# Splitting one head pair of the scores across the boundary of a woven cycle

## The chip, the cores and the metric

The kernel runs on one core of a Trainium2 chip. The metric is the device time of one execution in microseconds, the median of several runs. Before the change it is 1395.99 us (three runs, 1395.55 to 1398.74).

## The reference

A pre-norm transformer block on one sequence of 2048 tokens with width 512. Attention has 32 heads of 16 with a single key and value head shared by all; the feed-forward part is a gated GELU with 1792 hidden features. Everything is float32.

```python
q = (x @ wq).reshape(B, S, 32, 16).transpose(0, 2, 1, 3)
k = x @ wk
v = x @ wv
p = softmax(einsum("bhqd,bkd->bhqk", q, k) * 16 ** -0.5)
o = einsum("bhqk,bkd->bhqd", p, v).transpose(...).reshape(B, S, 512) @ wo

h = x + attention(layernorm(x))
h2 = h + (gelu(layernorm(h) @ w_gate) * (layernorm(h) @ w_up)) @ w_down
```

## The kernel before

**Blocks and groups.** The 2048 queries are worked in four blocks `b` of 512 columns. In a block the 32 heads come in eight groups `g` of four, and for each group the 2048 keys come in 16 chunks `kc` of 128. One iteration `i` is one (block, group, chunk): four heads, in two pairs `u = 0, 1`. There are 512 iterations and 1024 pairs, numbered by `n` (`i, u = divmod(n, 2)`).

**A score** (`scores`, L370): two matmuls, one for each head `a` of the pair. Each has 50 contraction rows, the first at partitions 0 to 49, the second at 64 to 113, so that the two stand in different row halves of TensorE and run at the same time. They write the two banks of one PSUM tile `s` (128 keys x 2 x 512 queries). ScalarE then takes the exponential of the whole tile, 1024 columns in one instruction (L374), into half of a tile `p` in SBUF. There are two `s` tiles (pool `pss`, four banks) in the woven part, and five `p` tiles.

**A weigh** (`weigh`, L378): for one iteration, four matmuls of 32 columns side by side multiply the four heads' `p` by the values and add to the accumulator `acc` (one bank). In the trace each of the four is two records. An iteration can be weighed when both of its exponentials are done. The list `pend` holds iterations that are scored but not yet weighed, and `finish(n)` weighs the `n` oldest.

**A dense step** (`step`, `rows`, L827): output projection, up projections and down projections of the block before the one in attention. Each product of 128 contraction rows is cut in two halves of 64 rows, the "firsts" in rows 0 to 63 and the "seconds" in rows 64 to 127, which go to different PSUM banks and are added by VectorE. A step issues one matmul of a first and one matmul of a second, which run at the same time; the seconds lag six steps behind (`LAG`). A product is mostly 12 steps long, so a product's half ends every six steps. When it ends, VectorE copies or adds its bank (`done`: L690, L694, L757, L615, L618), and up to two more VectorE instructions that wait in the list `later` are issued (`side`). There are three banks for products; two are in use at a time, and the list `spare` hands them out in the order in which they came free.

**The weave.** `CYCLES` sets the order by hand. A cycle has a number of weighs, all at its beginning, then a string of moves, `s` a score and `d` a dense step, and a second string for cycles in which too few dense steps are available (`idle`), where weighs and scores alternate:

```python
CYCLES = (
    (3, "ssdddddsdddsddds", "vssvssvs"),
    (3, "ssdddddsdddsddds", "vssvssvs"),
    (2, "ssdddddsdddsdddsddds", "ssvssvss"),
)
```

Three cycles make a repeat: 8 weighs, 16 scores, 36 dense steps. Before each cycle `before` issues what ScalarE and VectorE have to do beside it (the gate's tanh, L706; the divisions by the sums, L414; the turning of normalized rows). A tanh stands on ScalarE ahead of the cycle's exponentials. The order on TensorE, ScalarE and GpSimd is as written; SyncE and VectorE too in this part.

**What comes before and after.** The first block's attention and 23 scores of the second (`lead`) run without dense work; there a third tile `s3` serves the scores as well, and a few weighs alternate with scores. The last block's dense part follows the weave in an order of its own (L865).

Of the kernel before, what the change touches and what calls it, by code (L numbers as in the profile page):

```python
# [9 lines left out]
F32 = mybir.dt.float32  # L10
# [3 lines left out]
AF = mybir.ActivationFunctionType  # L14
# [5 lines left out]
P = 128  # L20
# [22 lines left out]
LAG = 6  # L43
# [16 lines left out]
def kernel(  # L60
# [12 lines left out]
    nc = tc.nc  # L73
# [6 lines left out]
    T = 512  # L80
# [8 lines left out]
    KR = 3 * DH + 2  # L89
    SCALE = float(DH) ** -0.5  # L90
# [21 lines left out]
    kaug = const.tile([P, S], F32R, name="kaug")  # L112
# [45 lines left out]
    def run(outer, first):  # L158
# [204 lines left out]
        def scores(i, p, qg, kc, u):  # L363

            third = width == 1 and (2 * i + u) % 3 == 2
            pool, tag, bufs = (ps, "s3", 1) if third else (pss, "s", 2)
            s = pool.tile([P, 2, T], F32, tag=tag, bufs=bufs, name=f"s_{i}_{u}")
            for a in range(2):
                rows = slice(64 * a, 64 * a + KR)
                nc.tensor.matmul(  # L370
                    s[:, a, :], kaug[rows, kc * P : (kc + 1) * P], qg[rows, u, :],
                    start=True, stop=True,
                )
            nc.scalar.activation(p[:, 2 * u : 2 * u + 2, :], s, AF.Exp, scale=SCALE)  # L374

        def weigh(acc, p, kc):
            for j in range(4):
# [84 lines left out]
        late = ExitStack()  # L462
# [95 lines left out]
        scaled_at, halves, gs, gated = {}, {}, {}, set()  # L558
# [246 lines left out]
        left = [0]  # L805
        built = []

        def rows(a):
            nonlocal at
            i = 0  # L810
            while i < len(queue):
                name, n, terms, done, ready = queue[i]
                i += 1
                if a == 0:
                    assert ready is None or ready()
                    left[0], at = n, i
                    built.append([])
                    source = iter(terms())
# [3 lines left out]
                for k in range(n):  # L822
                    if a == 0:
# [3 lines left out]
                    nc.tensor.matmul(  # L827
                        bank, lhsT[r], rhs[r], start=(k == 0), stop=(k == n - 1),
                        skip_group_check=True,
                    )  # L830
                    if k == n - 1:
                        spare.append(tag)
                        done(a, bank)
                        side(2)
                    yield

        def step(first=True):
            nonlocal ahead, clock
            clock += 1
            if first and next(firsts, 0) is None:  # L840
                ahead += 1
            if ahead > LAG or not first:
                assert ahead > 0
                next(seconds)
                ahead -= 1

        tail_banks = ["acc", "t3", "d", "d", "d", "t0", "t1", "t2"]

# [195 lines left out]

        cur = {}

        def score(n):

            nonlocal acc
            i, u = divmod(n, 2)  # L1050
            b, r = divmod(i, PER)
            g, kc = divmod(r, KC)
            if u == 0:
                if kc == 0:
                    cur["qg"] = qgs.pop((b, g))
                    acc = psa.tile([P, T], F32, tag="acc", bufs=1, name=f"acc_{b}_{g}")
                if kc == 2 and b * NG + g + 1 < NB * NG:
                    key = divmod(b * NG + g + 1, NG)
                    qgs[key] = load_q(*key)
                cur["p"] = sb.tile([P, 4, T], F32, tag="p", bufs=PB, name=f"p_{i}")  # L1060
            scores(i, cur["p"], cur["qg"], kc, u)
            if u == 1:
                pend.append((b, g, kc, cur["p"], acc, n))

        banks.close()
# [67 lines left out]
        assert not outs  # L1133
        set_banks("ps_rest")
# [7 lines left out]
        def before(idle):  # L1142
# [21 lines left out]
        fixed.enter_context(  # L1164
            tc.manual_schedule(engines={mybir.EngineType.SP, mybir.EngineType.DVE})
        )
        for i in range(-((lead - end) // 16)):
            if first and i in BOUND_LISTS:
                bound_flag(BOUND_LISTS.index(i))
            for count, woven, plain in CYCLES:  # L1170
                idle = available() < woven.count("d")
                if idle:
                    while available():
# [10 lines left out]
                for move in plain if idle else woven:  # L1184
                    if move == "d":
                        step()
                    elif move == "v":
                        if n == end and not last_x:
                            prepare_x()
                        finish(1)  # L1190
                        clock += 4
                    elif n < end:
                        score(n)
                        n += 1
                        clock += 1
        fixed.close()
        assert not pend and not outs and at == len(queue) and left[0] == 0
        held_banks.close()
# [383 lines left out]
```

## Time and profile before

| | |
|---|---|
| median of the runs | 1395.99 us |
| the profiled execution's own time | 1397.61 us |
| span in its trace | 1395.8 us |
| granted TensorE clock | 1.00 |
| weighs (L378), 4096 records | 490.0 us busy |
| scores (L370), 1984 records of the main shape | 388.3 us busy |
| exponentials (L374), 1024 | 959.6 us busy, 1037 ns each |
| tanh of the gate (L706), 42 | 27.8 us busy, 662 ns each |

The profile is a hardware trace of one execution. PE is TensorE's matmuls, PEld its weight loads, which overlap matmuls; DVE is VectorE, ACT ScalarE, POOL GpSimd. A row of the timeline has the start in us from the span's beginning, the time from the start of the first to the end of the last of the instructions merged in it, engine, line, operation, output and inputs, shapes, the count, and in brackets the idle time before it and what ended it. A row of a group has the busy time in all, the mean of one instruction in ns, and the idle time of the engine just before them with what ended most of it. Matmuls are pipelined: one of 512 columns is recorded with about 0.39 us, but the next can start before it ends, so the distance between starts tells the rate. Some matmul records may be missing.

### The profile page before, as it was taken

The page shows a single profiled execution, that of the slowest core. Times are in us where ns is not written, and L with a number is a line of the kernel's source. Part 1 is how long each engine was busy: PE and PEld are TensorE (multiplying, and loading weights), DVE is VectorE, ACT ScalarE, POOL GpSimd, SP SyncE. Part 2 cuts the span into 40 slices and gives each one's busy share as a digit, 9 for nine tenths or more (in the row PEclk, how much of TensorE's full clock was granted, in tenths as well). Part 3 has the DMA queues.
Part 4 walks back from the last instruction along what each step waited for, and adds up shares of the span by engine and source line. Part 5 has one row for each costly group of instructions (what it writes and reads, how often), then busy time and mean ns, then how long its engine had stood idle before and what let it go on. Part 6 is the DMA issues. An engine that isn't in the chain of part 4 may idle for free.

```text
span 1395.8 us, 25287 instructions
## 1 busy us (share of the span) xinstructions
PE 1379.5 (99%) x10406; PEld 753.3 (54%) x10406; DVE 651.0 (47%) x1097; ACT 1034.1 (74%) x1157; POOL 239.8 (17%) x346
## 2 busy tenths in 40 slices
PE   9999999999999999999999999999999999999998
PEld 7533333325555555545555555545555555558886
DVE  7413131314354444548364444448364453546665
ACT  8799999997787777877787777787778777772000
POOL 7576777621000000002000000001000000011000
PEclk9999999999999999999999999999999999999999
DMA  5565776753232333311522433321433333233552
GB/s 163 167 216 184 235 235 233 220 181 133 73 106 74 118 104 103 116 60 46 181 94 81 134 103 103 104 66 31 148 103 104 118 103 103 91 123 126 187 205 94
DMA packets 66783, 180.32 MB, mean 129 GB/s; under 512 B 9672, under 2 KB 9672, under 8 KB 66628
## 3 DMA queue, kind: packets, MB, share of 16 engines
q1 hardware_dynamic: 55324, 143.29, 31.0%
q0 software_dynamic: 10208, 35.26, 7.6%
q8 instruction: 84, 1.38, 0.4%
q14 instruction: 39, 0.32, 0.1%
q10 hardware_dynamic: 1128, 0.07, 0.1%
HBM read 130.87 MB, written 47.45 MB: 128 GB/s over the span
## 4 chain that ended last, share of the span: by engine, by line
PE 94%; ACT 2%; DMA 1%; DVE 1%; issue 1%; SPq 0%; POOL 0%; ACTq 0%; POOLq 0%
PE acc L378 33%; PE s L370 20%; PE pg L827 9%; PE pu L827 8%; PE pd L827 7%; PE pq L219 3%; PE pd L865 3%; PE pg L865 3%; PE pu L865 3%; PE pp L827 2%; ACT p L374 2%; PE pp L929 1%; PE pd_rest L877 1%; DMA x<-in_A_x_dram 1%; PE pk L1327 1%
## 5 line engine op out<-in xcount | busy, mean ns | idle before, releaser
L374 ACT ACTIVATE p<-s 128x1024 f32<-128x1024 f32 x1024 | 959.6, 1037 | 223.7 <-PE s L370 220.6
L378 PE MATMUL acc<-p,v_sb 128*32 128x512 f32 x4096 | 490.0, 598 | 0.0
L370 PE MATMUL s<-qg,kaug 50*128 50x512 f32 x1984 | 388.3, 426 | 4.2 <-ACT p L374 4.1
L370 PEld LDWEIGHTS s<-qg,kaug 50*128 50x128 f32 x1984 | 169.4, 184 | 281.7 <-ACT p L374 123.5
L378 PEld LDWEIGHTS acc<-p,v_sb 128*32 128x32 f32 x4096 | 108.7, 109 | 233.1 <-issue 218.7
L827 PE MATMUL pg<-x2h,w 64*128 64x512 f32 x672 | 175.2, 392 | 0.0
L827 PE MATMUL pu<-x2h,w 64*128 64x512 f32 x672 | 174.5, 392 | 0.0
L827 PE MATMUL pd<-w,gh 64*128 64x512 f32 x624 | 124.7, 394 | 1.9 <-DVE h L615 1.6
L757 DVE TENSOR_TENSOR h<-h,pd 128x512 f32<-128x512 f32 x80 | 55.0, 687 | 140.7 <-PE pd L827 140.6
L137 POOL TENSOR_SCALAR rstd<-mv 128x1 f32<-128x1 f32 x16 | 3.6, 223 | 649.1 <-DVE mv L135 648.8
L827 PEld LDWEIGHTS pg<-x2h,w 64*128 64x128 f32 x672 | 95.5, 186 | 11.4
L827 PEld LDWEIGHTS pu<-x2h,w 64*128 64x128 f32 x672 | 95.7, 186 | 10.8
L827 PE MATMUL pg<-x2l,w 64*128 64x512 f32 x336 | 99.9, 392 | 0.0
L827 PE MATMUL pu<-x2l,w 64*128 64x512 f32 x336 | 99.9, 391 | 0.0
L827 PEld LDWEIGHTS pd<-w,gh 64*128 64x128 f32 x624 | 69.7, 185 | 15.0 <-DVE h L615 2.5
L391 DVE COPY oT<-acc 128x512 f32<-128x512 f32 x32 | 22.1, 692 | 112.5 <-PE acc L378 112.3
L983 ACT ACTIVATE ga<-ga 128x512 f32<-128x512 f32 x14 | 8.8, 632 | 88.5 <-DVE ga L980 88.5
L827 PE MATMUL pd<-w,gl 64*128 64x512 f32 x312 | 72.1, 392 | 0.0
L694 DVE TENSOR_TENSOR g<-g,pg 128x512 f32<-128x512 f32 x42 | 28.8, 685 | 90.8 <-PE pg L827 90.8
L414 DVE RECIPROCAL oc<-oc 128x128 f32<-128x128 f32 x64 | 56.7, 923 | 21.4 <-DMA oc<-acc_d 17.6
L690 DVE COPY g<-pg 128x512 f32<-128x512 f32 x42 | 29.1, 692 | 72.0 <-PE pg L827 72.0
L694 DVE TENSOR_TENSOR u<-u,pu 128x512 f32<-128x512 f32 x42 | 28.8, 686 | 68.6 <-PE pu L827 68.6
(255 smaller groups left out, 1493.1 us busy)
## 6 DMA issues: line engine op xcount, KB each, us to landing
w<-w_d SPq DMA_DIRECT2D x126, 512.0 KB
w<-w_d SPq DMA_DIRECT2D x21, 1024.0 KB
qg<-q_d SPq DMA_DIRECT2D x62, 200.0 KB
q_d<-qh SPq DMA_DIRECT2D x32, 256.0 KB
acc_d<-oT SPq DMA_DIRECT2D x31, 256.0 KB
oc<-acc_d SPq DMA_DIRECT2D x124, 64.0 KB
w_d<-w_0b POOLq DMA_DIRECT2D x14, 512.0 KB, 4.6
w_d<-w_1b POOLq DMA_DIRECT2D x14, 512.0 KB, 3.4
```

The lines of the kernel that those rows point to most:

```text
L219: nc.tensor.matmul(pq, wt[c][:, d, :], xt[:, d, :], start=(n == 0), stop=(n == 3 * DC - 1),)
L370: nc.tensor.matmul(s[:, a, :], kaug[rows, kc * P : (kc + 1) * P], qg[rows, u, :], start=True, stop=True,)
L374: nc.scalar.activation(p[:, 2 * u : 2 * u + 2, :], s, AF.Exp, scale=SCALE)
L378: nc.tensor.matmul(acc[32 * j : 32 * j + 32, :], v_sb[:, kc, :], p[:, j, :], start=(kc == 0), stop=(kc == KC - 1), skip_group_check=True,)
L391: nc.vector.tensor_copy(oT, acc)
L414: nc.vector.reciprocal(oc[:, 1, sl], oc[:, 1, sl])
L690: nc.vector.tensor_copy(half, bank)
L694: nc.vector.tensor_tensor(half, half, bank, op=ALU.add)
L757: nc.vector.tensor_tensor(hs[b, t], hs[b, t], bank, op=ALU.add)
L827: nc.tensor.matmul(bank, lhsT[r], rhs[r], start=(k == 0), stop=(k == n - 1), skip_group_check=True,)
L865: nc.tensor.matmul(bank, lhsT, rhs, start=(i == 0), stop=(i == len(ts) - 1))
L877: nc.tensor.matmul(bank, lhsT, rhs, start=(i == 0), stop=(i == len(ts) - 1))
```

## The change

A cycle is now three numbers: weighs, scores and dense steps, and the strings are made from them by functions. Where it can, a cycle ends with one dense second and one single head: move `1` issues only the second of a step, and beside it head 0 of the next pair (rows 0 to 49), which goes to the dense products' third bank, the one not in use. The next cycle begins, after its weighs, with move `2`: only the first of a step, and beside it head 1 of that pair (rows 64 to 113), which goes to one half of an ordinary `s` tile. Each head then has an exponential of its own of 512 columns (L1118 of the changed kernel) instead of one of 1024 for both.

`choose` shifts the number of steps by up to two so that the last end of a product half falls four or five steps before the cycle's end. If that can't be had, or rows wait to be turned (`scaled_at`), or fewer than `EMPTY` moves have passed since the last end, or the next cycle has only two weighs and a tanh is due, the cycle ends with a whole step instead. The places of the scores among the steps are `WHOLE_AT` for a cycle that begins with two whole scores, and `HALF_AT` for one that begins with a half. The opening (`lead`) has one score more, 24.

The numbers in a repeat stay 8 weighs, 16 scores and 36 steps; the cycles' shares of scores and steps are 6 and 13, 5 and 12, 5 and 11.

```diff
 CYCLES = (
-    (3, "ssdddddsdddsddds", "vssvssvs"),
-    (3, "ssdddddsdddsddds", "vssvssvs"),
-    (2, "ssdddddsdddsdddsddds", "ssvssvss"),
+    (3, 6, 13),
+    (3, 5, 12),
+    (2, 5, 11),
 )
+WHOLE_AT, HALF_AT = (0, 1, 7, 11, 15, 19, 23), (1, 5, 9, 13, 17, 21)
+EMPTY = 5
...
-        def step(first=True):
+        def step(first=True, second=True):
             nonlocal ahead, clock
             clock += 1
             if first and next(firsts, 0) is None:
                 ahead += 1
-            if ahead > LAG or not first:
-                assert ahead > 0
+            if second and (ahead > LAG or not first) and ahead > 0:
                 next(seconds)
                 ahead -= 1
+        def choose(steps, half):
+            for more in (0, 1, -1, 2, -2):
+                if steps + more - last_end(steps + more, half) in (4, 5):
+                    return steps + more, True
+            return steps, False
+        def woven(pairs, steps, half, parted):
+            steps -= half
+            at, moves = (HALF_AT if half else WHOLE_AT)[:pairs], "2" * half
+            while pairs or steps:
+                if pairs and (len(moves) >= at[-pairs] or not steps):
+                    moves, pairs = moves + "s", pairs - 1
+                else:
+                    moves, steps = moves + "d", steps - 1
+            return moves + "1" * parted
...
+        def score_half(n, a):
+            if a == 0:
+                cur["open"] = open_pair(n)
+            i, u, b, g, kc = cur["open"]
+            if a == 0:
+                tag, s = take_bank(f"s_{i}_{u}_0")
+                spare.append(tag)
+            else:
+                s = pss.tile([P, 2, T], F32, tag="s", bufs=2, name=f"s_{i}_{u}_1")[:, 0, :]
+            score_head(s, cur["qg"], kc, u, a)
+            nc.scalar.activation(cur["p"][:, 2 * u + a, :], s, AF.Exp, scale=SCALE)
+            if a == 1 and u == 1:
                 pend.append((b, g, kc, cur["p"], acc, n))
...
-        n, lead = 0, 2 * PER + 23
+        n, lead = 0, 2 * PER + 24
...
-                if n % 4 == 2 and len(pend) > 2 and n < lead - 1:
+                if n % 4 == 2 and len(pend) > 2 and n < lead - 2:
                     finish(1)
-                elif n % 4 == 0:
+                elif n % 4 == 0 and n < lead:
                     finish(len(pend) - 2)
...
+                steps, parted = choose(steps, half)
+                parted = parted and not scaled_at and target < end
+                idle = available() < steps + parted
...
+                    elif move == "1":
+                        if scaled_at or clock - todo[2] < EMPTY or (after == 2 and tanhs):
+                            step()
+                        else:
+                            step(first=False)
+                            score_half(n, 0)
+                            half = True
+                    elif move == "2":
+                        step(second=False)
+                        score_half(n, 1)
+                        n, half = n + 1, False
```

`todo` holds how many matmuls the product in work has left on each side, and the move at which a product last ended; `last_end` works out from it where the last end in a cycle of so many steps would fall.

More of the change, by code (lines that the diff above doesn't have):

```diff
@@ L368, in scores, with score_head @@
             for a in range(2):
[L369 to L374, printed above, removed]
+                score_head(s[:, a, :], qg, kc, u, a)
+            nc.scalar.activation(p[:, 2 * u : 2 * u + 2, :], s, AF.Exp, scale=SCALE)
+        def score_head(s, qg, kc, u, a):
+            rows = slice(64 * a, 64 * a + KR)
+            nc.tensor.matmul(
+                s, kaug[rows, kc * P : (kc + 1) * P], qg[rows, u, :], start=True, stop=True
+            )
         def weigh(acc, p, kc):
@@ L805, in run @@
         left = [0]
+        todo = [0, 0, 0]
         built = []
@@ L841, in step, with last_end, plain @@
                 ahead += 1
-            if ahead > LAG or not first:
-                assert ahead > 0
+            if second and (ahead > LAG or not first) and ahead > 0:
                 next(seconds)
                 ahead -= 1
+        def last_end(steps, shift):
+            ends = [0]
+            for first, late in (
+                (todo[0] or 12, 0),
+                (todo[1] or 12 + max(LAG - ahead, 0), shift),
+            ):
+                ends += range(first + late, steps + 1, 12)
+            return max(ends)
+        def choose(steps, half):
[12 more added lines that the diff above has]
+            return moves + "1" * parted
+        def plain(count, pairs):
+            moves = "s" * (pairs - 2 * count)
+            for i in range(count):
+                moves += "v" + "s" * min(max(pairs - 2 * i, 0), 2)
+            return moves
         tail_banks = ["acc", "t3", "d", "d", "d", "t0", "t1", "t2"]
@@ L1045, in run, with open_pair @@
         cur = {}
-        def score(n):
+        def open_pair(n):
             nonlocal acc
@@ L1060, in score @@
                 cur["p"] = sb.tile([P, 4, T], F32, tag="p", bufs=PB, name=f"p_{i}")
+            return i, u, b, g, kc
+        def score(n):
+            i, u, b, g, kc = open_pair(n)
             scores(i, cur["p"], cur["qg"], kc, u)
             if u == 1:
+                pend.append((b, g, kc, cur["p"], acc, n))
+        def score_half(n, a):
[10 more added lines that the diff above has]
+            if a == 1 and u == 1:
                 pend.append((b, g, kc, cur["p"], acc, n))
@@ L1166, in run @@
         )
+        half, target = False, lead
         for i in range(-((lead - end) // 16)):
@@ L1169, in run @@
                 bound_flag(BOUND_LISTS.index(i))
-            for count, woven, plain in CYCLES:
-                idle = available() < woven.count("d")
+            for c, (count, pairs, steps) in enumerate(CYCLES):
+                target += pairs
+                after = CYCLES[(c + 1) % len(CYCLES)][0]
+                steps, parted = choose(steps, half)
+                parted = parted and not scaled_at and target < end
+                idle = available() < steps + parted
                 if idle:
+                    if half:
+                        score_half(n, 1)
+                        n, half = n + 1, False
                     while available():
@@ L1183, in run @@
                     later.extend(gate(*key))
-                for move in plain if idle else woven:
+                pairs = min(target, end) - n
+                moves = (
+                    plain(count, pairs)
+                    if idle
+                    else woven(pairs - half - parted, steps, half, parted)
+                )
+                for move in moves:
                     if move == "d":
@@ L1195, in run @@
                         clock += 1
+        assert not half
         fixed.close()
```

4 lines of the change are left out of this document (added).

## Prediction

> **What bounds the kernel now.** I read the page first, then the time by window, the timeline of a few cycles, the waits, and the groups by shape. TensorE is the bound, from the page's first part and its chain:
>
> ```profile
> PE 1379.5 (99%) x10406; PEld 753.3 (54%) x10406; DVE 651.0 (47%) x1097; ACT 1034.1 (74%) x1157; POOL 239.8 (17%) x346
> PE 94%; ACT 2%; DMA 1%; DVE 1%; issue 1%; SPq 0%; POOL 0%; ACTq 0%; POOLq 0%
> ```
>
> The change acts between about 352 and 1250 us, where scores, weighs and dense products are woven. The windows below are a long stretch of that stage and one repeat of its three cycles (busy time of PE, PEld, DVE, ACT, POOL in turn):
>
> ```profile
> 351.80:613.10 261.30, 261.30 (x2180) 145.21 (x2178) 123.29 (x193) 202.16 (x223) 0.00 (x0) 1.00 0.29 97
> 700.75:720.86 20.11, 20.11 (x171) 11.14 (x169) 13.69 (x22) 16.01 (x19) 0.00 (x0) 1.00 0.25 83
> ```
>
> PE is covered throughout, ACT works 16.0 of 20.1 us, so nothing is gained by feeding ACT as such. What can change is the length of PE's own slots. A slot is a pair of concurrent matmuls (both heads of a score, or both row halves of a dense step). Here is the start of the repeat's first cycle, after its weighs, from the timeline:
>
> ```profile
> 703.46 0.30 PEld L370 LDWEIGHTS s<-qg,kaug 50*128 50x128 f32 x4 [0.84 <-issue]
> 703.46 0.73 PE L370 MATMUL s<-qg,kaug 50*128 50x512 f32 x4
> 704.03 0.40 PE L827 MATMUL pu<-x2h,w 64*128 64x512 f32 x1
> 704.06 2.86 ACT L374 ACTIVATE p<-s 128x1024 f32<-128x1024 f32 x3 [1.53 <-PE s L370]
> 704.96 0.39 PE L827 MATMUL pu<-x2l,w 64*128 64x512 f32 x1
> 705.14 0.18 PEld L370 LDWEIGHTS s<-qg,kaug 50*128 50x128 f32 x2 [0.22 <-ACT p L374]
> 705.18 0.46 PE L370 MATMUL s<-qg,kaug 50*128 50x512 f32 x2
> 705.48 0.40 PE L827 MATMUL pg<-x2h,w 64*128 64x512 f32 x1
> ```
>
> Two scores take 0.57 us (0.34 with the weight load in the open, then 0.23), and four dense steps start from 704.03 to 704.96: 0.233 a slot. The third score should take that too, but the next step starts 0.30 after it. Its weight load waited for ACT to leave the score buffer: the first exponential ran from 704.06, and with the 1.037 of the group's row below it ended at 705.10, so the load came 0.04 later. In the repeat's second cycle the same place is free of loss:
>
> ```profile
> 709.31 0.73 PE L370 MATMUL s<-qg,kaug 50*128 50x512 f32 x4
> 709.85 1.94 ACT L374 ACTIVATE p<-s 128x1024 f32<-128x1024 f32 x2 [1.10 <-PE s L370]
> 709.88 0.40 PE L827 MATMUL pu<-x2h,w 64*128 64x512 f32 x2
> 710.80 0.39 PE L827 MATMUL pg<-x2h,w 64*128 64x512 f32 x1
> 710.93 0.19 PEld L370 LDWEIGHTS s<-qg,kaug 50*128 50x128 f32 x2 [0.16 <-ACT p L374]
> 711.27 0.40 PE L827 MATMUL pg<-x2l,w 64*128 64x512 f32 x1
> ```
>
> In both, the slot after a late-loaded score starts 0.34 after its load (705.14 to 705.48, 710.93 to 711.27). As a slot is 0.235 long, a score planned at time t loses: load + 0.105 - t, if that is positive. The load starts 0.05 after the exponential that frees its buffer. Only the first exponential after the weighs matters; the later ones follow each other 0.91 apart ((2.86 - 1.04) / 2 from the row at 704.06), and the scores 0.93 to 0.94 (four slots).
>
> **The change part by part.** Work: the order holds the same weighs, matmuls and cycles (146 groups of weighs, 13 of them with a single weigh, in both). A half score shares its slot with a half step, so no slot is added. Counted in the order, 109 of about 132 woven cycles end with a lone head, and as many begin with the other.
>
> What stands on PE around the end of a cycle in block 0's dense stage, before (s is a score, pg and pu the up projections with their row half, acc the weighs):
>
> ```order
> L827 MATMUL pg_1_1_3968<-x2h_3257,w_0_1_0_3269 128x512
> L370 MATMUL s_0_3987<-qg_2_3565,kaug 128x512 x2
> L378 MATMUL acc_2_3903<-p_3904,v_sb 32x512 x4
> L378 MATMUL acc_2_3903<-p_3928,v_sb 32x512 x4
> L378 MATMUL acc_2_3903<-p_3962,v_sb 32x512 x4
> L370 MATMUL s_1_4005<-qg_2_3565,kaug 128x512 x2
> L370 MATMUL s_0_4010<-qg_2_3565,kaug 128x512 x2
> L827 MATMUL pu_1_0_4014<-x2h_3257,w_0_1_1_3885 128x512
> ```
>
> And in the changed kernel, where s_1_0 and s_1_1 are the two heads of one pair:
>
> ```order
> L835 MATMUL pg_1_1_3974<-x2l_3258,w_0_1_0_3269 128x512
> L378 MATMUL s_1_0_3988<-qg_2_3554,kaug 128x512
> L384 MATMUL acc_2_3894<-p_3895,v_sb 32x512 x4
> L384 MATMUL acc_2_3894<-p_3916,v_sb 32x512 x4
> L384 MATMUL acc_2_3894<-p_3955,v_sb 32x512 x4
> L835 MATMUL pg_1_0_3945<-x2l_3258,w_0_1_0_3269 128x512
> L378 MATMUL s_1_1_4006<-qg_2_3554,kaug 128x512
> L378 MATMUL s_0_4010<-qg_2_3554,kaug 128x512 x2
> L835 MATMUL pg_1_0_3945<-x2h_3257,w_0_1_0_3269 128x512
> ```
>
> The weighs stand between two half slots now, and the second score after them comes three dense steps after the first full one instead of five. It takes the buffer that the lone second head used, so it waits for that head's short exponential. ACT's order at the same place, before (ga is the gate's tanh):
>
> ```order
> L374 ACTIVATE p_3962<-s_1_3974 128x1024
> L374 ACTIVATE p_3986<-s_0_3987 128x1024
> L706 ACTIVATE ga_0_3887<-ga_0_3887 128x512
> L374 ACTIVATE p_3986<-s_1_4005 128x1024
> L374 ACTIVATE p_4009<-s_0_4010 128x1024
> ```
>
> and after:
>
> ```order
> L374 ACTIVATE p_3980<-s_0_3981 128x1024
> L1118 ACTIVATE p_3980<-s_1_0_3988 128x512
> L712 ACTIVATE ga_0_3891<-ga_0_3891 128x512
> L1118 ACTIVATE p_3980<-s_1_1_4006 128x512
> L374 ACTIVATE p_4009<-s_0_4010 128x1024
> ```
>
> One exponential of 1024 columns has become two of 512, one on each side of the weighs and of the tanh. These are ACT's groups by shape from which I size it:
>
> ```profile
> L374 ACT ACTIVATE p<-s 128x1024 f32<-128x1024 f32 x1024 | 959.6, 1037 | 223.7 <-PE s L370 220.6
> L706 ACT ACTIVATE ga<-ga 128x512 f32<-128x512 f32 x42 | 27.8, 662 | 0.0
> L1351 ACT ACTIVATE vT<-pk 128x512 f32<-128x512 f32 x4 | 2.3, 570 | 0.0
> L965 ACT ACTIVATE hp<-pp 128x512 f32<-128x512 f32 x4 | 2.1, 624 | 0.0
> ```
>
> *The new wait.* Call the first weight load after the weighs 0. By the rows at 709.31 the head's exponential starts at 0.54 and lasts d. The first full score is at 0.34, the three steps at 0.57, 0.80 and 1.04, the score in question at 1.27. It loses 0.54 + d + 0.05 + 0.105 - 1.27 = d - 0.575. The same formula gives the third score of the cycle at 703.46 a loss of 0.60 + 1.04 + 0.155 - 1.73 = 0.06, as seen. No row has an exponential of 512 columns; d is bounded by the copy out of PSUM (0.570: no loss) and the tanh (0.662: 0.087). I take 0.60, the middle of the two rows that read PSUM and write float32 as this does (0.570 and 0.624). Loss 0.025, times 109: **+2.7 us**, with ends 0 and +9.5. The scores behind it don't wait: the full exponential starts at 0.54 + 0.60 - 0.125 = 1.02 and frees its buffer for a score that may then start at 2.21 and is planned at 2.23.
>
> The Trainium skill (ScalarE: Activation LUTs, "What ACT_TABLE_LOAD costs") gives an activation with immediate scale and bias 186 ns and 0.833 ns an element, so splitting one pays the 186 ns twice. For 1024 columns that is an estimate of 1039 ns, and this trace agrees with 1037. For 512 it is an estimate of 613 ns, by which this term would be 4.1 us and not 2.7.
>
> *ACT's extra work.* Two halves follow each other 0.475 apart each where one took 0.91: 0.04 more at d = 0.60, 0.16 at 0.662, 4 to 18 us in all. It is hidden in the 1.10 and 1.53 us that ACT sits idle under each group of weighs (rows above).
>
> *What goes.* The 0.07 of the third score occurs once a repeat, 43 repeats: 2.8 us. In addition the last score of some cycles takes longer, because the weighs wait for an exponential that is just being finished; here one such and one without:
>
> ```profile
> 720.48 0.45 PE L370 MATMUL s<-qg,kaug 50*128 50x512 f32 x2
> 720.86 0.64 PE L378 MATMUL acc<-p,v_sb 128*32 128x512 f32 x4
> ...
> 707.13 0.39 PE L370 MATMUL s<-qg,kaug 50*128 50x512 f32 x2
> 707.45 0.64 PE L378 MATMUL acc<-p,v_sb 128*32 128x512 f32 x4
> ```
>
> 0.38 against 0.32; seen in about half of the repeats, so 22 x 0.06 = 1.2 us. In the new order at least four more slots lie between a pair and its weigh, so it ends. Of the 4.0 us together the 109 of 132 cycles get rid of: **-3.3 us**.
>
> *The lead.* One score moves from the weave to the opening before it. There ACT sets the pace (rows before 310.20, where the weave begins):
>
> ```profile
> 308.45 0.91 PE L370 MATMUL s<-qg,kaug 50*128 50x512 f32 x4
> 309.77 0.51 PE L370 MATMUL s<-qg,kaug 50*128 50x512 f32 x2 [0.42 <-ACT p L374]
> 310.20 1.06 PE L378 MATMUL acc<-p,v_sb 128*32 128x512 f32 x8
> ```
>
> A third score before the weighs waited for ACT; a fourth adds 0.91 there and saves a slot of 0.23 later: **+0.7 us**. On PE, before and after:
>
> ```order
> L378 MATMUL acc_0_3191<-p_3324,v_sb 32x512 x4
> L370 MATMUL s_0_3364<-qg_0_2944,kaug 128x512 x2
> L370 MATMUL s_1_3368<-qg_0_2944,kaug 128x512 x2
> L370 MATMUL s_0_3373<-qg_0_2944,kaug 128x512 x2
> L378 MATMUL acc_0_3191<-p_3337,v_sb 32x512 x4
> ```
>
> ```order
> L384 MATMUL acc_0_3191<-p_3324,v_sb 32x512 x4
> L378 MATMUL s_0_3364<-qg_0_2944,kaug 128x512 x2
> L378 MATMUL s_1_3368<-qg_0_2944,kaug 128x512 x2
> L378 MATMUL s_0_3373<-qg_0_2944,kaug 128x512 x2
> L378 MATMUL s_1_3377<-qg_0_2944,kaug 128x512 x2
> L384 MATMUL acc_0_3191<-p_3337,v_sb 32x512 x4
> ```
>
> The fourth score is all that differs.
>
> *The borrowed bank.* The lone first head waits for VectorE to empty the bank of the product that ended last; the weighs stand behind it on PE. By count it comes 7 to 9 slots after that end, 1.65 to 2.1 us, with its load 0.1 before. VectorE took this long, once free and once busy:
>
> ```profile
> 705.92 0.69 DVE L694 TENSOR_TENSOR g<-g,pg 128x512 f32<-128x512 f32 x1 [2.99 <-PE pg L827]
> ...
> 711.51 0.39 PE L827 MATMUL pu<-x2h,w 64*128 64x512 f32 x1
> ...
> 712.46 0.68 DVE L694 TENSOR_TENSOR u<-u,pu 128x512 f32<-128x512 f32 x1
> ```
>
> That is 1.13 us after the matmul at 705.48, and 1.63 after the one at 711.51. Only the second, met by a head 7 slots on (30 of the 109), would cost about 0.15: between 0 and 4.5 us, and as the first kind is the common one, **+0.5**. The next product takes the bank after the weighs (1.7 us or more later), when the head's exponential is done.
>
> Sum: 2.7 - 3.3 + 0.7 + 0.5 = +0.6 us. The profiled execution took 1397.6 with a span of 1395.8; it becomes 1398.2. That execution lies 1.6 above the median of 1396.0, so the median becomes 1396.6.
>
> **The rivals.** *Slower: the second score waits.* If the short exponential is nearer to the tanh's 0.662, or starts at 0.60 as at 703.46, each begun cycle loses up to 0.087, and the sum is 9.5 - 3.3 + 0.7 + 0.5 = +7.4: 1403.4. It passes +4.2 us from d = 0.633. For it: the exponential of 1024 takes 1.037, more than twice 0.5, so its fixed part isn't small. Against it: both PSUM readers are shorter.
>
> *Faster: the products' own waits go.* The dense products wait for VectorE in places, by the view of line 827:
>
> ```profile
>   DVE h L615: 4.1, 4
>   DVE u L694: 1.4, 3
>   DVE h L757: 0.8, 4
> ```
>
> The new planner places the last end of a product four or five steps before the weighs, which gives VectorE time. If all 6.3 us go, the sum is -5.7: 1390.3. Against it: L615's waits stand where blocks change, and the planner doesn't touch those.
>
> *Much faster: ACT sets the pace.* ACT waited 220.6 us for scores (its row above). If that were the bound, half an exponential more under each of 109 groups of weighs would bring 0.5 x 109 = 54 us: 1342. Both window rows speak against it. That the change doesn't happen is excluded by the order: 109 lone heads stand there.
>
> **How the numbers follow.** Forecast 0.57; slower rival 0.23; faster rival 0.17; ACT's pace 0.03. 0.3%, or 4.2 us, is about what a measurement can tell from no change. Slower by more takes the slower rival and a little of the forecast: 0.25. Faster by more: 0.20. Within: 0.55. The range reaches from near the faster rival to near the slower one: 1391.0 to 1402.5.
>
> **What would show it.** Right: woven repeats still near 20.1 us; the short exponential about 0.60; the score after the first full one with its load near 1.19 after the first load, its slot about 0.26; no score of 0.38 before weighs. Wrong: that slot at 0.30 or more in most cycles (slower rival), a wait for VectorE ahead of the lone head (the borrowed bank), or repeats shorter by more than 0.1 us, which nothing here explains.

## The result, and the profile after

The changed kernel takes 1411.77 us (median of five runs, 1411.31 to 1413.22) against 1395.99 before. The ratio is 1.011, with a 95% interval of 1.0095 to 1.0125. The change makes the kernel 1% slower; the forecast was 1396.6 with a range up to 1402.5. The profiled execution took 1411.48 us and has a span of 1409.8, 14.0 longer than before.

On the page the changed kernel looks much the same. These are its first line of engines and its chain:

```profile
PE 1390.5 (99%) x10406; PEld 744.4 (53%) x10406; DVE 653.6 (46%) x1097; ACT 1041.1 (74%) x1266; POOL 240.6 (17%) x346
PE 91%; DVE 3%; ACT 2%; DMA 1%; issue 1%; POOL 1%; SPq 0%; DVEq 0%; POOLq 0%; ACTq 0%
```

PE is still busy for 99%: most of the added time is booked as busy PE (1390.5 us for 1379.5, with the same matmuls). The chain tells more: PE gave up three points, two of them to DVE, which did almost the same work as before.

To find the place, both spans are cut where equal numbers of weighs are done. Each row has the stretch, its length, and the busy time and count of the weighs alone. Before:

```profile
310.20:351.81 41.61, 15.60 (x128) 3.34 (x128) 1.00 0.42 150
351.81:592.74 240.93, 89.85 (x768) 21.44 (x769) 1.00 0.31 100
592.74:694.08 101.34, 37.85 (x320) 8.69 (x321) 1.00 0.27 93
694.08:915.45 221.37, 82.37 (x704) 19.61 (x704) 1.00 0.33 105
915.45:1015.61 100.16, 38.08 (x324) 8.59 (x324) 1.00 0.23 79
1015.61:1236.90 221.29, 82.35 (x705) 19.67 (x706) 1.00 0.32 103
```

After:

```profile
310.98:353.36 42.38, 15.60 (x128) 3.24 (x129) 1.00 0.42 156
353.36:596.01 242.65, 89.86 (x768) 21.28 (x768) 1.00 0.31 99
596.01:700.88 104.87, 37.86 (x321) 8.67 (x321) 1.00 0.27 90
700.88:923.50 222.62, 82.37 (x704) 19.51 (x705) 1.00 0.33 103
923.50:1027.30 103.80, 38.06 (x320) 8.56 (x320) 1.00 0.22 79
1027.30:1250.00 222.70, 82.41 (x708) 19.55 (x710) 1.00 0.32 101
```

The weave begins 0.8 us later (310.98 for 310.20). Its opening is 0.8 longer. The three long steady stretches are 1.7, 1.2 and 1.4 longer, 4.3 together. The two short stretches, in which one block's dense work ends and the next one's output projection begins, are 3.5 and 3.6 longer. They hold under a quarter of the weave's time and half of the loss. The last 0.9 us of the spans' difference come behind the last row.

**In a steady cycle.** The start of a half-begun cycle, from the timeline of the changed kernel:

```profile
710.93 0.29 PEld L378 LDWEIGHTS s<-qg,kaug 50*128 50x128 f32 x3
711.50 0.60 ACT L1118 ACTIVATE p<-s 128x512 f32<-128x512 f32 x1 [1.17 <-PE s L378]
711.98 0.39 PE L835 MATMUL pg<-x2h,w 64*128 64x512 f32 x1
711.99 1.02 ACT L374 ACTIVATE p<-s 128x1024 f32<-128x1024 f32 x1
712.15 0.19 PEld L378 LDWEIGHTS s<-qg,kaug 50*128 50x128 f32 x2 [0.22 <-ACT p L1118]
712.21 0.44 PE L378 MATMUL s<-qg,kaug 50*128 50x512 f32 x2
712.49 0.40 PE L835 MATMUL pu<-x2h,w 64*128 64x512 f32 x1
```

The short exponential lasts 0.60, ends at 712.10, and the second full score's load comes 0.05 later, at 1.22 from the first load. Its slot is 0.28 long (712.21 to 712.49). This is the forecast's new wait, with its releaser in the bracket, in 108 cycles; the slots' excess over 0.2335 adds up to 5.3 us.

**At a change of block.** The timeline around 644, and the wait in front of a lone head:

```profile
641.29 2.53 DVE L655 STREAM_TRANSPOSE xt<-xb 32x128 f32<-32x128 f32 x8
643.41 0.39 PE L835 MATMUL pp<-wo_hi,o_lo 64*128 64x512 f32 x1
643.85 0.69 DVE L624 TENSOR_TENSOR h<-h,pp 128x512 f32<-128x512 f32 x1
...
644.59 0.18 PEld L378 LDWEIGHTS s<-qg,kaug 50*128 50x128 f32 x1 [1.22 <-DVE h L624]
644.59 0.50 PE L378 MATMUL s<-qg,kaug 50*128 50x512 f32 x1 [0.79 <-DVE h L624]
645.02 0.16 PEld L384 LDWEIGHTS acc<-p,v_sb 128*32 128x32 f32 x8 [0.25 <-issue]
```

The lone head's dense partner starts at 643.41, the head itself at 644.59, and the weighs stand behind it. It waits for the bank of an output projection, which VectorE empties (L624) only after eight transposes, 2.53 us in one piece. The waits of TensorE by line and releaser (us in all, times, longest) have no such rows for scores before the change:

```profile
PE s L378 <- DVE h L624: 1.6, 2, 0.8
PE s L378 <- DVE h L763: 0.6, 1, 0.6
```

By the slots ahead of lone heads there are five such places, all where blocks change, with 3.2 us in all: four behind an output projection (L624) and one behind a down projection (L763). A late head also takes a slot of its own instead of sharing its partner's: from the partner's start to the weighs it is 1.61 us here (643.41 to 645.02) where a head in time takes 0.33. Counted so, the five places cost 4.9 us.

### The profile page after: what moved, and what is told of

Its sections match the earlier page's. It is cut to its first block, busy times and chain, and to the rows that moved or that the text cites. A ratio compares the mean times of both kernels' runs of the same rounds, so it can differ in the third digit from the quotient of the medians.

```text
span 1409.8 us, 25424 instructions
## 1 busy us (share of the span) xinstructions
PE 1390.5 (99%) x10406; PEld 744.4 (53%) x10406; DVE 653.6 (46%) x1097; ACT 1041.1 (74%) x1266; POOL 240.6 (17%) x346
## 4 chain that ended last, share of the span: by engine, by line
PE 91%; DVE 3%; ACT 2%; DMA 1%; issue 1%; POOL 1%; SPq 0%; DVEq 0%; POOLq 0%; ACTq 0%
PE acc L384 32%; PE s L378 18%; PE pu L835 9%; PE pg L835 9%; PE pd L835 8%; PE pq L223 3%; PE pd L904 3%; PE pg L904 3%; PE pu L904 3%; ACT p L374 2%; PE pp L835 1%; DVE xt L655 1%; PE pp L968 1%; PE pd_rest L916 1%; PE pk L1410 1%
## 5 line engine op out<-in xcount | busy, mean ns | idle before, releaser
L374 ACT ACTIVATE p<-s 128x1024 f32<-128x1024 f32 x915 | 858.9, 1041 | 57.1 <-PE s L378 54.3
L378 PE MATMUL s<-qg,kaug 50*128 50x512 f32 x1984 | 425.9, 427 | 8.0 <-ACT p L374 5.4
L378 PEld LDWEIGHTS s<-qg,kaug 50*128 50x128 f32 x1984 | 186.9, 184 | 214.2 <-ACT p L374 122.5
L1118 ACT ACTIVATE p<-s 128x512 f32<-128x512 f32 x218 | 135.3, 622 | 172.5 <-PE s L378 139.1
L835 PE MATMUL pu<-x2h,w 64*128 64x512 f32 x672 | 207.6, 399 | 0.0
L835 PE MATMUL pg<-x2h,w 64*128 64x512 f32 x672 | 198.8, 396 | 0.0
L835 PEld LDWEIGHTS pu<-x2h,w 64*128 64x128 f32 x672 | 102.4, 186 | 41.6 <-issue 33.5
L763 DVE TENSOR_TENSOR h<-h,pd 128x512 f32<-128x512 f32 x80 | 54.9, 686 | 146.0 <-PE pd L835 123.1
L835 PE MATMUL pd<-w,gh 64*128 64x512 f32 x624 | 121.5, 396 | 0.7 <-DVE h L621 0.7
L835 PEld LDWEIGHTS pg<-x2h,w 64*128 64x128 f32 x672 | 98.4, 186 | 24.1 <-issue 15.9
L835 PE MATMUL pg<-x2l,w 64*128 64x512 f32 x336 | 104.6, 395 | 0.0
L835 PE MATMUL pu<-x2l,w 64*128 64x512 f32 x336 | 100.7, 393 | 0.0
L835 PEld LDWEIGHTS pd<-w,gh 64*128 64x128 f32 x624 | 71.0, 186 | 22.1 <-issue 10.1
L835 PE MATMUL pd<-w,gl 64*128 64x512 f32 x312 | 80.5, 399 | 0.0
L835 PEld LDWEIGHTS pg<-x2l,w 64*128 64x128 f32 x336 | 49.6, 186 | 15.2 <-issue 8.4
```

Of the source, the lines that this page charges most:

```text
L378: nc.tensor.matmul(s, kaug[rows, kc * P : (kc + 1) * P], qg[rows, u, :], start=True, stop=True)
L763: nc.vector.tensor_tensor(hs[b, t], hs[b, t], bank, op=ALU.add)
L835: nc.tensor.matmul(bank, lhsT[r], rhs[r], start=(k == 0), stop=(k == n - 1), skip_group_check=True,)
L1118: nc.scalar.activation(cur["p"][:, 2 * u + a, :], s, AF.Exp, scale=SCALE)
```

## The experiments

Each run has the kernel before beside it on the same chip; differences are against that run's own 1395.9 to 1397.5 us. By this measure the change costs 15.8 us. The theory after the result: three causes add up, the second score's wait on the short exponential, the lone heads that wait at changes of block, and scores that stand too close together for ACT. The main rival: the weave has one limit, and a wait that is removed at one place comes back at another.

**1. The second score one step later**, in half-begun cycles with four full scores.

```diff
             at, moves = (HALF_AT if half else WHOLE_AT)[:pairs], "2" * half
+            if half and pairs == 4:
+                at = 1, 6, 10, 14
```

> The changed kernel, but in cycles that begin with a half and have four whole scores the second score comes four dense steps after the first instead of three (66 cycles in the order). Theory (it waits 0.05 us for the lone second head's exponential, 0.622 us long): the wait is gone in 66 of 108 cycles, 66 x 0.05 = 3.2 us, so 1408.6 us. Rival (the half slots themselves cost the time, whatever follows them): no change, 1411.8.

Measured: 1410.42 us, ratio 1.0097 (1.0081 to 1.0112), 13.9 over the kernel before instead of 15.8. The medians alone can't separate this from no gain; the steady stretches can:

```profile
355.10:597.02 241.92, 89.86 (x768) 21.26 (x769) 1.00 0.32 99
702.10:923.96 221.86, 82.37 (x704) 19.49 (x705) 1.00 0.32 104
1028.03:1249.89 221.86, 82.37 (x704) 19.49 (x704) 1.00 0.31 102
```

They are 0.7, 0.8 and 0.8 shorter than in the changed kernel, 2.3 together. By slots, the wait fell by 3.0 us there (90 cycles with it became 33). So it was a real loss, most of which comes back when it is taken away.

**2. No lone head after an output projection.**

```diff
-                        todo[2] = clock
+                        todo[2] = clock + 100 * name.startswith("pp")
```

> The changed kernel, but no lone head is scored while the product that ended last is an output projection; the cycle ends with a whole step there (100 lone heads instead of 109). Theory (at the two block changes the lone head waits for VectorE to empty the projection's bank, with the weighs behind it, about 4.5 us in all, and the whole-ended cycles in their place cost about 1): 3 to 4 us less, 1408. Rival (VectorE is late there anyway, so the next product waits instead, as one did for 1.2 us in the kernel before): no change, 1411.8.

Measured: 1408.63 us, ratio 1.0087 (1.0074 to 1.0101). The two stretches with changes of block, same weighs as above:

```profile
596.05:699.06 103.01, 37.85 (x320) 8.65 (x320) 1.00 0.26 92
921.87:1024.01 102.14, 38.06 (x320) 8.54 (x320) 1.00 0.23 81
```

They are 1.9 and 1.7 us shorter than in the changed kernel; the steady stretches change by less than 0.2 each. This holds half of what the changes of block lost, and the rival fails: no product waits for VectorE's projection adds in the heads' place. The late head behind a down projection stays. The changes of block still cost 3.7 us more than before.

**3. No lone head at all**, with the planner's shares and shifts kept.

```diff
-                parted = parted and not scaled_at and target < end
+                parted = False
```

> The changed kernel with its planner and its shares of 6, 5, 5 scores, but no lone heads: every cycle begins with two whole scores. Theory (each late weight load of a score costs by the formula load + 0.105 - plan): 0.06 us in two of three cycles, and 0.15 in the cycle of six scores, where the last comes three slots after the one before: 43 x (0.12 + 0.15) = 11.6 us against 3 in the kernel before, with 0.8 for the opening: 1396.0 + 9.4 = 1405. Rival (the lone heads are the whole cost): 1397.

Measured: 1409.30 us, ratio 1.0092 (1.0076 to 1.0107), over both expectations: 12.8 over the kernel before, without a single lone head. The steady stretches, same weighs as above:

```profile
352.59:596.06 243.47, 89.86 (x769) 21.27 (x769) 1.00 0.30 98
699.50:922.92 223.42, 82.36 (x704) 19.49 (x704) 1.00 0.32 103
1024.12:1247.72 223.60, 82.37 (x705) 19.49 (x705) 1.00 0.32 101
```

Against the kernel before, they are 6.9 longer, more than with lone heads (4.3); the opening is 0.0 longer, the changes of block 3.2. By slots, the third score now waits 0.06 in 68 of 102 steady cycles (35 before). The sixth score of a cycle, three slots behind the fifth, is late too, as here:

```profile
416.57 4.69 ACT L374 ACTIVATE p<-s 128x1024 f32<-128x1024 f32 x5 [1.52 <-PE s L378]
...
419.61 0.40 PE L378 MATMUL s<-qg,kaug 50*128 50x512 f32 x2
...
420.39 0.18 PEld L378 LDWEIGHTS s<-qg,kaug 50*128 50x128 f32 x2 [0.36 <-ACT p L374]
```

It was due three slots after 419.61, at 420.31, and its load comes at 420.39 for ACT: by the formula 0.18 late. The ends of these 34 cycles cost 0.17 each, 5.8 us. So the new shares (6, 5 and 5 scores on 13, 12 and 11 steps) and their places cost by themselves. The lone heads win 2.6 us of it back in the steady part and lose 4.0 at the changes of block and 0.8 in the opening. The rival, that they are the whole cost, is refuted.

**4. The kernel before with its third score later** in the cycle where it waits 0.06.

```diff
-    (3, "ssdddddsdddsddds", "vssvssvs"),
+    (3, "ssddddddsdddsdds", "vssvssvs"),
```

> The kernel before with one string altered: in the second cycle of each repeat the third and fourth scores come one dense step later and the last one stays (ssddddddsdddsdds). Theory (in that cycle the third score's load is 0.06 us late; one slot later it is in time, and the fifth needs only the third's exponential, which is done): 43 x 0.06 = 2.6 us less, 1393.4. Rival (ACT's pace sets the scores, so the fifth, three slots after the fourth, waits instead): no change or slower, 1396 to 1399.

Measured: 1396.41 us beside 1396.49, ratio 0.9996 (0.9985 to 1.0007): no change that the medians can tell, to about 1.5 us. The steady stretches of its trace are 0.9 shorter. The edited cycle, from its first score:

```profile
702.63 0.30 PEld L370 LDWEIGHTS s<-qg,kaug 50*128 50x128 f32 x4 [0.84 <-issue]
...
703.23 4.70 ACT L374 ACTIVATE p<-s 128x1024 f32<-128x1024 f32 x5 [1.53 <-PE s L370]
...
704.36 0.19 PEld L370 LDWEIGHTS s<-qg,kaug 50*128 50x128 f32 x2
...
706.16 0.19 PEld L370 LDWEIGHTS s<-qg,kaug 50*128 50x128 f32 x2 [0.20 <-ACT p L374]
```

The third score's load (704.36) no longer waits, but the last one's (706.16) does. ACT's five exponentials run without a gap (4.70 us): the last score takes the buffer of the third exponential, which ends at 703.23 + 2 x 0.91 + 1.04 = 706.09. Of the 2.9 us that the third scores give back, 1.9 return at the cycles' ends. The rival has the wait right.

**5. The shares of the kernel before**, with lone heads.

```diff
-    (3, 6, 13),
-    (3, 5, 12),
-    (2, 5, 11),
+    (3, 5, 11),
+    (3, 5, 11),
+    (2, 6, 14),
```

> The changed kernel with the shares of the kernel before: cycles of 5, 5 and 6 scores and 11, 11 and 14 steps in place of 6, 5, 5 and 13, 12, 11; lone heads and the place of the second score as in the changed kernel. Theory (ACT's chain inside a cycle): the sixth score of an 18-slot cycle with 3 weighs waits, because its buffer is free only after 1.02 + 2 x 0.91 + 1.04 + 0.05 from the first weight load, while the score is planned at 3.84; the cycles of six scores now have 19 slots and no such wait, so the crowded scores of the changed kernel (about 2.5 us over those of the kernel before) go: 1409.3 us. Rival (the loss is in the planner's shifts and the lone heads themselves, spread over all cycles): no change, 1411.8.

Measured: 1416.60 us, ratio 1.0135 (1.0118 to 1.0152), 19.1 over the kernel before, against both expectations. The interval overlaps that of the change, but the steady stretches are 2.1 longer than in the changed kernel and the changes of block as much. The planner takes one or two steps from some cycles to place an end, and in 12 cycles two scores now stand one step apart:

```profile
433.17 0.19 PEld L378 LDWEIGHTS s<-qg,kaug 50*128 50x128 f32 x2
433.33 0.40 PE L378 MATMUL s<-qg,kaug 50*128 50x512 f32 x2
433.56 0.39 PE L835 MATMUL pu<-x2l,w 64*128 64x512 f32 x2
434.09 0.29 PEld L378 LDWEIGHTS s<-qg,kaug 50*128 50x128 f32 x3 [0.57 <-ACT p L374]
434.43 0.39 PE L835 MATMUL pu<-x2h,w 64*128 64x512 f32 x1
```

From the step at 433.56 to the score are 0.53, and from the score to the next step 0.34: 0.40 lost in one place, for ACT. By its slots the cycle loses 0.35 more than its neighbours, and 12 x 0.35 = 4.2 us. What was meant to spread the scores crowded them; the rule (a score waits until the exponential two scores back has left its buffer) is supported, my reading of the order was not.

**6. The same, with every second score one step later.**

```diff
-WHOLE_AT, HALF_AT = (0, 1, 7, 11, 15, 19, 23), (1, 5, 9, 13, 17, 21)
+WHOLE_AT, HALF_AT = (0, 1, 7, 11, 15, 19, 23), (1, 6, 10, 14, 18, 22)
```

> As the run with the old shares, and the second score after a half-begun start stands one dense step later in every such cycle (places 1, 6, 10, 14, 18). Theory: the wait of 0.05 in each of about 108 cycles goes too (5.3 us in the changed kernel's trace), and no new one comes, since ACT's chain from the second score on is as before and the later scores keep their places: 1404.0 us. What is left over the kernel before (about 7.5) is then the changes of block, the lead and the opening of the weave. Rival (waits are only handed on to the end of the cycle, as when the third score of the kernel before was put later): 1408 to 1409.

Measured: 1413.30 us, ratio 1.0112 (1.0095 to 1.0128). The absolute number missed for the reason just told. The step from run 5, beside the same runs of the kernel before, is -3.3 us against 5.5 of waits that went from the slots: about 60% come home, and waits of later scores are 1.6 us longer.

**7. The second score one step earlier**, the suspected wait made larger.

```diff
-WHOLE_AT, HALF_AT = (0, 1, 7, 11, 15, 19, 23), (1, 5, 9, 13, 17, 21)
+WHOLE_AT, HALF_AT = (0, 1, 7, 11, 15, 19, 23), (1, 4, 9, 13, 17, 21)
```

> The changed kernel with the second score after a half-begun start one dense step earlier (place 4 in place of 5), in about 108 cycles. Theory (it waits for the lone head's short exponential; its loss is d - 0.575 with d = 0.622, and 0.2335 more when it is planned one slot earlier): 108 x 0.2335 = 25 us more, less about 2 us for the cycles of 18 slots, whose last score no longer waits: 1435 us. Rival (the slot of 0.28 has another reason than that exponential): 1411 to 1414.

Measured: 1432.30 us, ratio 1.0248 (1.0231 to 1.0265), 34.8 over the kernel before and 19.0 more than the changed kernel; 23 were expected, the rival said 0 to 2. A cycle's start:

```profile
718.47 0.29 PEld L378 LDWEIGHTS s<-qg,kaug 50*128 50x128 f32 x3
719.03 0.60 ACT L1118 ACTIVATE p<-s 128x512 f32<-128x512 f32 x1 [1.17 <-PE s L378]
719.29 0.38 PE L835 MATMUL pg<-x2l,w 64*128 64x512 f32 x1
719.68 0.19 PEld L378 LDWEIGHTS s<-qg,kaug 50*128 50x128 f32 x2 [0.44 <-ACT p L1118]
720.02 0.40 PE L835 MATMUL pu<-x2h,w 64*128 64x512 f32 x1
```

The load comes at 1.21 from the first, as in the changed kernel, although the score is planned 0.2335 earlier: what sets it is the short exponential, and the next step follows 0.34 later. By its slots the cycle loses 0.23 more than in the changed kernel. That this exponential holds the second score up is shown.

**8. The kernel before with a split exponential**, the first of each cycle, TensorE's order untouched.

```diff
-            nc.scalar.activation(p[:, 2 * u : 2 * u + 2, :], s, AF.Exp, scale=SCALE)
+            for a in range(2) if first_of[0] else ():
+                nc.scalar.activation(p[:, 2 * u + a, :], s[:, a, :], AF.Exp, scale=SCALE)
+            if not first_of[0]:
+                nc.scalar.activation(p[:, 2 * u : 2 * u + 2, :], s, AF.Exp, scale=SCALE)
+            first_of[0] = False
...
+                first_of[0] = not idle and n < end
```

> The kernel before, with nothing changed but the exponential of the first score of each of 135 woven cycles: two of 512 columns, one behind the other, in place of one of 1024. TensorE's order is the same. Theory (inside a cycle ACT's chain is as tight as PE's slots): with 0.622 a half and a pitch of about 0.50, the buffer comes free 0.08 later and everything behind it too, in some 131 cycles: 10.5 us more, 1407. Rival (ACT is idle for 4 us of each repeat of 20.1 and takes it up there): 1396 to 1398.

Measured: 1403.43 us beside 1395.92, ratio 1.0059 (1.0045 to 1.0073): 7.5 us more.

```profile
705.57 0.30 PEld L372 LDWEIGHTS s<-qg,kaug 50*128 50x128 f32 x4 [0.84 <-issue]
706.17 1.08 ACT L377 ACTIVATE p<-s 128x512 f32<-128x512 f32 x2 [1.50 <-PE s L372]
707.14 2.87 ACT L379 ACTIVATE p<-s 128x1024 f32<-128x1024 f32 x3
707.31 0.19 PEld L372 LDWEIGHTS s<-qg,kaug 50*128 50x128 f32 x2 [0.28 <-ACT p L377]
```

The two halves keep ACT for 0.97 until the next exponential starts (706.17 to 707.14) where one took 0.91. The third score's load comes 1.74 after the first load; in the cycle at 703.46 of the kernel before it was 1.68. The waits of third scores rise from 3.0 us to 10.2 (135 cycles, 0.075 each), although ACT then has some 4 us of idle time in a repeat. The forecast of 10.5 had a pitch of 0.50 for the half (0.485 measured) and forgot that a third of the cycles waited already. At a cycle's start, ACT is as tight as PE.

**9. Both mends at once**: all second scores later (run 6's line) and no lone head after a projection (run 2's line), on the changed kernel.

> The changed kernel with two mends at once: the second score after a half-begun start one dense step later in every such cycle, and no lone head in the moves behind an output projection. Theory (two separate causes, which add up): the one by itself brought 3.1 us, the other 3.3 in the runs with the old shares, of 15.5 in all: 1405.5. What is left, 9 us, is then crowded last scores (cycles in which two scores stand one or two steps apart), the lead and the opening. Rival (the waits are the same ones seen at two places): 1408 or more.

Measured: 1406.19 us, ratio 1.0074 (1.006 to 1.0088): 10.3 over the kernel before, 5.5 better than the change, nearer to the theory than to the rival. The two causes together are a third of the loss. Two thirds stay, and run 3 has a loss of that size without a lone head. No version that was run is measurably faster than the kernel before.

## Why the prediction was wrong

**The term that is missing.** The sum came to +0.6 us, and 15.8 were measured. The step that failed first is the one that begins with "Work": it counts the same weighs, matmuls and cycles and finds that "no slot is added", and the sum has no term for the new shares and the places of the whole scores. "Only the first exponential after the weighs matters" rules the later scores out. Run 3 has these shares and shifts without any lone head, and is 12.8 us slower: scores later in the cycle come before ACT has left their buffer. With lone heads it is 15.8, so the heads, for which nearly all of the priced terms stand, add about 3 on balance. Shares and heads don't simply add up, though: with heads other scores are crowded. Nor did the count of slots hold: a lone head that is late can't share its partner's slot.

The terms that the sum does have, one by one, as the changed kernel shows them:

**The new wait** was forecast with its mechanism, its score and its count (109 cycles; 108 seen), at 2.7 us; it is 5.3. The duration was right: at the starts of cycles the short exponential has 0.60. What failed in this term is the start: "the head's exponential starts at 0.54" was read from a cycle that begins with a full score. In a half-begun cycle it starts 0.57 after the first load, in the mean of 108 cycles; that the dense first's load stands ahead of the head's is the likely reason, not shown. With that the formula gives d - 0.55 = 0.05, which is what was measured, and run 7 shows the releaser. The page of the Trainium skill (ScalarE: Activation LUTs, "What ACT_TABLE_LOAD costs") gave an estimate of 613 ns. The group's row has a mean of 622, over first heads that queue behind other exponentials (0.66 in the timeline) and second ones that don't (0.60):

```profile
L374 ACT ACTIVATE p<-s 128x1024 f32<-128x1024 f32 x915 | 858.9, 1041 | 57.1 <-PE s L378 54.3
L1118 ACT ACTIVATE p<-s 128x512 f32<-128x512 f32 x218 | 135.3, 622 | 172.5 <-PE s L378 139.1
```

The estimate lies between the two; its 4.1 us was nearer than 2.7, but the difference came from the start and not from the duration. The prediction's "pays the 186 ns twice" agrees roughly with the recorded durations (run 8: two of 0.60 for one of 1.04), but not with the pace, which is what counts here: 0.97 for 0.91.

**What goes** was -3.3. The waits of third scores fell by 1.8 us (3.0 to 1.3). The long last slots were sized about right: 27 of 130 woven cycles before the change end with 0.36 to 0.38 instead of 0.32 or 0.33, some 1.3 us in all; after it five do, while others end later still, crowded or with a late head. But "the scores behind it don't wait" was worked out for the first scores of a cycle only. In the cycles of 18 slots the last two full scores stand two steps apart, and the last one's buffer isn't free by then; these crowded scores cost 1.7 us in the steady stretches, so that most of what went came back. "It is hidden", of ACT's extra work, failed as well where run 8 could test it: at the start of a cycle a split costs time, although ACT is idle under the weighs.

**The lead** was +0.7; the weave begins 0.8 later. Right. That the opening behind it would be 0.8 longer wasn't seen; run 3 shows that it goes when no lone head is made.

**The borrowed bank** was +0.5, with ends 0 and 4.5. It is the largest miss among the priced terms. The wait was sized from two adds of the up projections, 1.13 and 1.63 us after their matmul. It was looked for in 30 of 109 cycles and sits in five: where blocks change and VectorE is busy with other things first, such as eight transposes ahead of the projection's add. The prediction even had the waits for a projection's add (L615; the heads wait for its neighbour, L618 before and L624 now) in hand and put them aside, because "the planner doesn't touch those". It doesn't move them, but it puts a lone head, and with it a whole group of weighs, behind them. Lone heads behind output projections cost 3.6 us by run 2 (12.1 over the kernel before instead of 15.8). The changes of block cost 7.2 in all, and 3.2 of that stand in run 3 without any lone head.

**The rivals.** The slower rival had the right first half: the second score waits in every begun cycle. Its point of decision was put at d = 0.633; d of 0.598 with a start 0.025 later costs as much as d = 0.623, below that point. The weave's start, the opening and the steady stretches come to 5.9 us, which is near the range's upper end by themselves; the changes of block carried the result out. The faster rival's waits for VectorE grew instead of going. ACT's pace as a bound for all is refuted by the lengths of the steady stretches. In its weaker form, that ACT's chain within a cycle is as tight as PE's, it is shown by runs 3, 4 and 8, and that form was missing. By slots the kernel before loses some 3 us to late third scores; run 4, the only run that moved them, won back 1.0 of it by slots and nothing that shows in the median.

**What stays open.** With lone heads after projections taken out, the changes of block still cost 3.7 us more than before, and 3.2 with none at all. In run 3 1.4 of them are dense products that wait longer for the projection's add: 3.0 us at two places (`PE pd L835 <- DVE h L621`) for 1.6 before (`PE pd L827 <- DVE h L615`). The rest may be scores that crowd where the planner cuts cycles short, as in run 5, but no run took only that away. Nor did a run put lone heads into the hand-made order of the kernel before, so what they would cost there isn't known. Some 1.2 us of the steady loss are spread over more than a thousand slots of under 0.015 each, and have no name. The medians differ by 15.8 us where the spans differ by 14.0, since the profiled execution before lay 1.6 above its median.

## What to carry to other kernels

When two engines take turns over a few buffers, ask how long the other one's chain is within one cycle, not over the span: ACT was 74% busy here and yet 0.06 us more of it at a cycle's start came out as 0.05 us of every cycle. A resource that is borrowed from another producer is priced by the worst queue of the engine that frees it, and by what stands behind the waiter: one lone head held up a whole group of weighs. A change that re-cuts a cycle needs a price for the new cut too, and a run without the idea itself, only with the new cut, gives it: here that was 12.8 of 15.8 us. And a start offset from a row of another kind of cycle is an assumption: 0.025 us of it was half of a term here.

## What the runs showed of the hardware

Splitting an activation was cheaper than its two durations say: two of 512 columns took 0.97 until the next could start, where one of 1024 took 0.91, though their recorded durations are 0.60 each. The recorded duration isn't the same everywhere, either. In the changed kernel a short exponential that starts alone has 0.60 (112 of them), and one that stands right behind another instruction has 0.65 in the mean (106), up to 0.66. But the second halves of run 8 stand behind a short one and have 0.59, so the queue alone doesn't explain it.
